# A decaying-attention and two-layer feed-forward kernel on one core: a wider window of loads under way, a state sum moved to a later unit, and a one-product mark for a bank

## The chip, the cores and the metric

The kernel runs on one core of one Trainium2 chip. The metric is the device time of one execution in microseconds (us), given as the median of several runs. One execution was also taken with the hardware profiler, and all rows below come from it. The core's engines work side by side and each takes its instructions in the order in which they are written: TensorE (PE, with PEld for its weight loads), VectorE (DVE), ScalarE (ACT), GpSimd (POOL) and SyncE (SP), which here only issues transfers (DMA).

## The reference, cut to what matters

```python
# attention with decay, per head, in 12 chunks of 64 positions
intra = einsum('bhic,bhjc->bhij', qb, kb) * Dmask            # "scores", masked
intra = einsum('bhij,bhjd->bhid', intra, vb)
inter = einsum('bhid,bhde->bhie', qb * lam_pow, kv_state)
out[:, :, sl] = intra + inter
kv_state = lam_block * kv_state + einsum('bhsd,bhse->bhde', kb * rev_pow, vb)
...
x = out.transpose(0, 2, 1, 3).reshape(1536, 512)
h = x @ w_in;   x = maximum(0.01 * h, h) @ w_out             # 512 -> 2048 -> 512
h = x @ w_in2;  solu = h * softmax(h)                        # 512 -> 1024
y = layernorm(solu) * g_ln @ w_out2                          # 1024 -> 512
```

Everything is float32; the weights come to the kernel as 64-bit words, which it takes apart on the chip.

## The kernel before, in words

**Attention.** The 12 chunks are steps `s` = 0 to 11, two batches together. A step has four groups of 64x64 products on PE: `scores_mm` (line 196), `state_mm` (210), `xs_mm` (250: masked scores times values) and `xq_mm` (264: queries times the state). DVE masks the scores (`scores_ev`, 204) and adds the new state sum to the decayed old state (`state_ev`, 236, reading PSUM bank `aps1`, which is also called `kb`). POOL scales queries (165) and decays the state (190). `alone` writes one group, `both` writes two groups product by product in turn. Steps 0 to 3 run before the feed-forward layer begins; step 4 runs inside its unit 7, step 5 in unit 10 and so on.

**Feed-forward layer 1.** A unit `u` is (token block of 512, feature block of 128). `l1_mm` (439) makes the 128x512 block of h in bank `hps0` or `hps1` by 12 products; `l1_split` puts the leak on it (ACT, 442) and splits it into a high part `ghi` (ACT, 445) and a low part `glo` (DVE, 447); `l2_mm` (456) multiplies both with `w_out` into four banks `acc` by 12 products. PE alternates l1 of unit i and l2 of unit i-1. Scores of the next step are put into the `hps` bank that the next unit's l1 will write.

**Weights.** Pair `n` is one feature block of `w_in` ("IN" half) and the one before it of `w_out` ("OUT" half), 512 KB each. In the first 17 units the pairs are loaded and taken apart while PE uses them. Per pair ACT does `word_hi` (350), `word_lo` (354) and `high` (409); DVE does `clamp` (360), `shift` (370), `join` (379) and `low` (428). In unit i from 4 on the pieces are written so that DVE does clamp and shift of pair i+2, low of pair i+1, `glo` of unit i, then join of pair i+2, and ACT does high of pair i+1, the two steps of `l1_split`, then the words of pair i+3. l1 of unit i needs high and low of pair i.

**Loads.** All weight loads are issued by SP, in order. `load` lets a load go only when, with it, no more than `limit` bytes are under way: it walks back over the earlier loads until their sum exceeds the limit, and waits for that one. Two constants give limits, `AHEAD` (2 MB) and `CALM` (1 MB); loads for attention (`ldw`, `qk`, `kv`) always use `AHEAD`. A load also waits for the readers of the buffer that it fills.

**The mark.** In step 3 the last `xq_mm` of a bank and the first `xs_mm` of it add into the same bank from other rows of the array. `see` therefore lets PE write a few columns of another bank after the `xq_mm` of a bank, lets ACT copy one column of that (244), and `xs_mm` waits for the copy.

`busy(n)` is n products of constants that nobody reads.

Of the kernel before, what the change touches and what calls it, by code (L numbers as in the profile page):

```python
# [10 lines left out]
U32 = mybir.dt.uint32  # L11
# [5 lines left out]
P = 128  # L17
CH = 64
NPAIR = 4
NB = 2  # L20
NPRE = 4
# [3 lines left out]
AHEAD, CALM = 1 << 21, 1 << 20  # L25
# [3 lines left out]
NF = FF1 // P  # L29
# [15 lines left out]
def fused_kernel(ctx: ExitStack, tc: tile.TileContext, att, vt, tab, cst, w_in, w_out, w_in2, w_out2, out):  # L45
# [7 lines left out]
    pe, dve, act, pool, sync = nc.tensor, nc.vector, nc.scalar, nc.gpsimd, nc.sync  # L53
# [10 lines left out]
    aps = [pp.tile([P, 512], F32, name=f"aps{i}") for i in range(2)]  # L64
# [19 lines left out]
    def rows(h):  # L84

        return HALF[1 - h]

    def jrows(s, h):

        return HALF[h] if s < NPRE else HALF[1 - h]  # L90
# [5 lines left out]
    def at(bank, rows, b, pr):  # L96

        if isinstance(bank, tuple):
            return bank[b][rows, pr * CH : (pr + 1) * CH]
        return bank[rows, (b * NPAIR + pr) * CH : (b * NPAIR + pr + 1) * CH]  # L100
# [12 lines left out]
    def load(queue, out, in_, limit=AHEAD):  # L113

        size = 4
        for n in out.shape:
            size *= n
        ins = queue.dma_start(out=out, in_=in_).ins
        ahead = size
        for before, n in reversed(flight):  # L120
            ahead += n
            if ahead > limit:
                tc.add_manual_dep(ins, before.name, SYNC, reason="bytes under way")
                break
        flight.append((ins, size))
# [66 lines left out]
    def scores_mm(s, bank, b, pr):  # L192
        q, k = (qk_t[s][:, :, 0], qk_t[s][:, :, 1]) if s >= NPRE else ld[s][0:2]
        for h in range(2):
            d = rows(h)
            pe.matmul(at(bank, jrows(s, h), b, pr), k[d, b, pr], q[d, b, pr], start=True, stop=True)  # L196
# [41 lines left out]
    LASTPRE, seen, mark = NPRE - 1, {}, tabs[:, 0:NB]  # L238

    def see(s, b):  # L240
        c = (b * NPAIR + NPAIR) * CH - 1
        bank = (aps, hps)[b][0]
        scores_mm(s, bank, b, NPAIR - 1)
        seen[b] = act.copy(mark[:, b : b + 1], bank[:, c : c + 1]).ins

    def xs_mm(s, bank, b, pr):
# [27 lines left out]
    def each_pair(*groups):  # L274

        for pr in range(NPAIR):
            for mm, s, bank, b in groups:
                mm(s, bank, b, pr)

    def alone(mm, s, bank):  # L280
        for b in range(NB):
            each_pair((mm, s, bank, b))

    def both(mm, s, bank, mm2, s2, bank2):
        for b in range(NB):
            each_pair((mm, s, bank, b), *([(mm2, s2, bank2, b)] if s2 < NS else []))

    def step(s, xbank, kbank, rbank):

        both(xs_mm, s, xbank, state_mm, s if s < NS - 1 else NS, kbank)  # L290
        both(xq_mm, s, xbank, scores_mm, s + 1, rbank)
# [5 lines left out]
    def x_hi(s, bank):  # L297
        for src, dst in parts(bank, x_place(s, xhi)):
            act.copy(dst, src)

    def x_lo(s, bank):
        for src, dst, hi in parts(bank, x_place(s, xlo), x_place(s, xhi)):
            dve.tensor_tensor(dst, src, hi.bitcast(F32), op=ALU.subtract)
# [8 lines left out]
    def whole(n):  # L312

        return IN if n == 0 else OUT if n == NF else BOTH

    def load_weights(n, halves=None):
        if n >= len(order):
            return
        kind, f = order[n]
        if n not in raws:  # L320
            if n == NF:
                raws[n] = tmp.tile([P, 1, 512, 2], U32, tag="s", name="rawl")
            else:
                raws[n] = wp.tile([P, 2, 512, 2], U32, tag="w", name="raww")
        t = raws[n]
        if kind == "a":
            load(sync, out=t.rearrange("p h a b -> p (h a b)"), in_=w_in2[f].bitcast(U32))
            return
        halves = halves or whole(n)
        for i in range(halves.start, halves.stop):  # L330
            src = w_out2[f + i] if kind == "b" else w_out[f - 1] if i else w_in[f]
            load(sync, out=t[:, 0 if n == NF else i].rearrange("p a b -> p (a b)"), in_=src.bitcast(U32), limit=(CALM // 2 if n == 1 and i else CALM) if n else AHEAD)

    def of(n, halves):

# [38 lines left out]
    def join(n, halves=None):  # L374
        if n >= len(order):
            return
        raw, x = of(n, halves)
        xu = x.bitcast(U32)
        dve.scalar_tensor_tensor(xu, xu, 0x80000000, raw[:, :, 0], op0=ALU.bitwise_and, op1=ALU.bitwise_or)  # L379
# [19 lines left out]
    def high(n, halves=None):  # L399
        if n >= len(order):  # L400
            return
        kind, f = order[n]
        halves = halves or whole(n)
        t, x = pieces(n), xs_t[n]
        if kind == "b":
            for i in range(2):
                act.activation(t[:, 0, i], x[:, i], AF.Copy, scale=gln[:, f + i : f + i + 1])
        else:
            act.copy(t[:, 0, halves], x[:, halves])  # L409
# [23 lines left out]
    def l1_mm(u, bank):  # L433
        b, f = u
        w = win_t[f].rearrange("p s (k c) -> p s k c", k=KD)
        groups = ((0, xhi), (1, xhi), (0, xlo)) if u == (0, 0) else ((0, xhi), (0, xlo), (1, xhi))
        terms = [(s, k, x) for s, x in groups for k in range(KD)]
        for i, (s, k, x) in enumerate(terms):
            pe.matmul(bank, w[:, s, k], x[b][:, k], start=(i == 0), stop=(i == len(terms) - 1))  # L439
# [136 lines left out]
    c1 = nc.const_aps.tensor(1.0, (P, 1), BF16)  # L576
# [3 lines left out]
    def busy(n):  # L580
        for _ in range(n):
            pe.matmul(aps[0], c1.to_broadcast([P, P]), c1.to_broadcast([P, 512]), start=True, stop=True)
# [30 lines left out]
    xb, sb, kb = acc[0:2], acc[2:4], aps[1]  # L613
# [47 lines left out]
    x3 = (xb[1], hps[1])  # L661
    for b in range(NB):
        each_pair((xq_mm, 3, x3, b))
        see(3, b)
    join(1, IN)
    x_lo(2, xb[0])
    both(xs_mm, 3, x3, state_mm, 3, kb)
    busy(1)
    x_hi(3, x3)
    high(1, IN)  # L670
    x_lo(3, x3)
# [42 lines left out]
    for i, u in enumerate(items[1:], 1):  # L714
        bank = hps[i % 2]
        s = step_at.get(i)
        spare = hps[(i + 1) % 2]
        if i > 1:
            if i == 5:
                alone(scores_mm, NPRE, aps[0])  # L720
            l1_mm(u, bank)
            if s is not None:
                step(s, aps[0], aps[1], spare)
        if i == 2:
            join(3, IN)
            high(3, IN)
            clamp(3, OUT)
            low(3, IN)
            shift(3, OUT)
            l1_split(u, bank)  # L730
            words(4, IN)
            join(3, OUT)
            high(3, OUT)
            clamp(4, IN)
            shift(4, IN)
            low(3, OUT)
            words(4, OUT)
            join(4, IN)
            high(4, IN)
            clamp(4, OUT)  # L740
            shift(4, OUT)
            low(4, IN)
            word_hi(5)
            join(4, OUT)
            word_lo(5)
        elif i == len(items) - 1:
            h2_norm(1, second=lambda: l1_split(u, bank))
        elif i > 2:
            part = OUT if i == 3 else None
            high(pair_at(i, 1), part)  # L750
            clamp(pair_at(i, 2))
            shift(pair_at(i, 2))
            low(pair_at(i, 1), part)
            l1_split(u, bank)
            if s is not None:
                scores_ev(s + 1, spare)
            if i == 6:
                scores_ev(NPRE, aps[0])
                scale_q(NPRE, pool)
                scale_k(NPRE, act)  # L760
            if s is not None:
                state_ev(s, aps[1])
                x_hi(s, aps[0])
                x_lo(s, aps[0])
                load_kv(s + 1)
                load_qk(s + 2)
                scale_q(s + 1, pool)
                decay_state(s + 1, pool)
            if i - 1 in step_at:
                scale_k(step_at[i - 1] + 1, act)  # L770
            join(pair_at(i, 2))
            if i == 4:
                state_ev(NPRE - 1, kb)
            words(pair_at(i, 3))
        load_weights(pair_at(i, 5))
        if i == 2:
            load_kv(NPRE)
            load(sync, out=fix, in_=cst)
            load_qk(NPRE + 1)
        if i == len(items) - 3:  # L780
            h2_norm(0)
            ln_turn(0, on_act=())
        l2_mm(items[i - 1])
        if items[i - 1][1] == NF - 1:
            l2_split(items[i - 1][0])
        if i in h2_after:
            h2_mm(h2_after[i])
# [84 lines left out]
```

## Time and profile before

| what | value |
|---|---|
| median of 3 runs | 447.06 us (445.94 to 447.09) |
| the profiled execution | 445.46 us, span 443.7 us |
| PE busy | 433.7 us (98% of the span) |
| DVE, ACT, POOL busy | 267.3, 195.6, 32.0 us |
| TensorE clock granted | 1.00 (2.4 GHz) in all slices |

The span runs from the first to the last instruction; the profiled execution's own time is 1.8 us longer. A row of a timeline gives the start, the length, the engine, the line of kernel.py, the operation, its output and input tiles, and in brackets how long the engine sat idle before it and what ended that. Rows of equal instructions that follow each other are merged (x12).

### The profile page before, as it was taken

Reading aid. Unit: us, or ns where it says so; the run is one execution under the profiler, and the core shown is the slowest. Engines: PE = TensorE matmul, PEld = TensorE weight load, DVE = VectorE, ACT = ScalarE, POOL = GpSimd, SP = SyncE. Lnnn points to the kernel's source line nnn. Section 1 sums busy time; section 2 is a strip of 40 time slices with the busy share of each in tenths; the row PEclk is TensorE's granted clock in tenths of the full one; section 3 lists DMA queues with packets and bytes.
Section 4 is the critical chain, followed back from the end, with each engine's and each line's share of the span. In section 5 each row is a group of like instructions: output and inputs, shape, how many; then the busy total and the mean of one; then the engine's idle time right before and its main releaser. Section 6 shows DMA issues by size and latency. Waiting matters only on the chain.

```text
span 443.7 us, 8024 instructions
## 1 busy us (share of the span) xinstructions
PE 433.7 (98%) x3270; PEld 356.8 (80%) x3272; DVE 267.3 (60%) x423; ACT 195.6 (44%) x332; POOL 32.0 (7%) x38
## 2 busy tenths in 40 slices
PE   8899998999999999999999999999999999999996
PEld 4788777888888888888888888888888888888886
DVE  4898989999541121211133889716779877777640
ACT  4587866977443222222234778512424322222221
POOL 1500102102201020100000000000000000000000
PEclk9999999999999999999999999999999999999999
DMA  8678788883302030100025542000112222222111
GB/s 296 231 255 260 243 246 236 252 235 98 97 11 87 0 98 0 49 1 0 1 95 188 191 189 96 1 1 10 38 37 72 88 75 73 75 72 74 58 47 47
DMA packets 23699, 46.85 MB, mean 106 GB/s; under 512 B 4336, under 2 KB 12016, under 8 KB 23152
## 3 DMA queue, kind: packets, MB, share of 16 engines
q1 hardware_dynamic: 21792, 44.78, 31.4%
q10 hardware_dynamic: 1872, 1.58, 1.3%
q8 instruction: 25, 0.41, 0.4%
q14 instruction: 10, 0.08, 0.1%
HBM read 37.95 MB, written 3.15 MB: 93 GB/s over the span
## 4 chain that ended last, share of the span: by engine, by line
PE 83%; ACT 0%; issue 0%; DVE 0%
PE acc L456 25%; PE hps L439 25%; PE acc L568 15%; PE aps L476 6%; PE hps L476 5%; PE acc L476 4%; PE aps L250 1%; PE aps L264 1%; PE hps L196 0%; PE aps L210 0%; PE aps L536 0%; PE acc L536 0%; ACT osb L571 0%; DVE state L225 0%
## 5 line engine op out<-in xcount | busy, mean ns | idle before, releaser
L439 PE MATMUL hps<-xhi,wio 128*128 128x512 f32 x384 | 102.9, 390 | 2.7 <-DVE r L204 1.2
L447 DVE TENSOR_TENSOR glo<-hps,ghi 128x512 fp32r<-128x512 f32 x48 | 33.1, 689 | 110.9 <-ACT ghi L445 110.7
L456 PE MATMUL acc<-ghi,wio 128*128 128x512 f32 x384 | 96.1, 392 | 0.6 <-ACT ghi L445 0.6
L439 PEld LDWEIGHTS hps<-xhi,wio 128*128 128x128 f32 x384 | 71.8, 188 | 18.3 <-ACT raww L354 1.6
L456 PEld LDWEIGHTS acc<-ghi,wio 128*128 128x128 f32 x384 | 71.4, 188 | 16.1 <-ACT ghi L445 1.0
L442 ACT ACTIVATE hps<-hps 128x512 f32<-128x512 f32 x48 | 28.0, 584 | 104.9 <-PE hps L439 104.9
L568 PE MATMUL acc<-wb,ln 128*128 128x512 f32 (+1 forms) x312 | 67.6, 373 | 0.0
L568 PEld LDWEIGHTS acc<-wb,ln 128*128 128x128 f32 x312 | 55.3, 188 | 10.2
L439 PE MATMUL hps<-xlo,wio 128*128 128x512 f32 x192 | 51.3, 389 | 0.0
L456 PE MATMUL acc<-glo,wio 128*128 128x512 f32 x192 | 51.3, 389 | 0.0
L439 PEld LDWEIGHTS hps<-xlo,wio 128*128 128x128 f32 x192 | 36.0, 188 | 7.5
L456 PEld LDWEIGHTS acc<-glo,wio 128*128 128x128 f32 x192 | 36.0, 188 | 7.5
L350 ACT ACTIVATE x<-raww 128x1024 f32<-128x1024 f32 (+1 forms) x28 | 27.8, 995 | 11.7 <-DMA raww<-in_w_in_dram 6.6
L379 DVE SCALAR_TENSOR_TENSOR x<-x,raww 128x1024 uint32<-128x1024 uint32 (+1 forms) x28 | 32.2, 1152 | 0.1
L370 DVE SCALAR_TENSOR_TENSOR raww<-x,raww 128x1024 uint32<-128x1024 uint32 (+1 forms) x28 | 29.6, 1056 | 3.8 <-ACT raww L354 1.7
L445 ACT CAST ghi<-hps 128x512 fp32r<-128x512 f32 x48 | 28.2, 587 | 1.5
L354 ACT ACTIVATE raww<-raww 128x1024 uint32<-128x1024 uint16 (+1 forms) x28 | 27.9, 998 | 0.0
L509 POOL TENSOR_TENSOR small<-small,nhalf 128x1 f32<-128x1 f32 x12 | 6.6, 549 | 234.5 <-DVE small L508 234.5
L428 DVE TENSOR_TENSOR wio<-x,wio 128x1024 fp32r<-128x1024 f32 (+1 forms) x21 | 22.2, 1057 | 1.5 <-ACT wio L409 1.5
L409 ACT CAST wio<-x 128x1024 fp32r<-128x1024 f32 (+1 forms) x21 | 17.8, 849 | 11.2 <-DVE x L379 11.2
L165 POOL TENSOR_TENSOR qk<-qk,qpow 128x512 f32<-128x512 f32 x8 | 11.6, 1445 | 140.4 <-PE hps L196 109.6
L571 ACT COPY osb<-acc 128x512 f32<-128x512 f32 (+1 forms) x13 | 7.2, 555 | 32.3 <-PE acc L568 19.5
(115 smaller groups left out, 494.6 us busy)
## 6 DMA issues: line engine op xcount, KB each, us to landing
raww<-in_w_out_dram SPq DMA_DIRECT2D x23, 512.0 KB, 4.3
raww<-in_w_in_dram SPq DMA_DIRECT2D x16, 512.0 KB, 4.3
qk<-in_att_dram SPq DMA_DIRECT2D x8, 512.0 KB, 4.6
raww<-in_w_in_dram SPq DMA_DIRECT2D x4, 1024.0 KB, 4.8
lt<-e SPq DMA_DIRECT2D x124, 32.0 KB, 1.8
out_dram<-osb SPq DMA_DIRECT2D x11, 256.0 KB, 2.2
ldw<-in_att_dram SPq DMA_DIRECT2D x7, 384.0 KB, 5.4
kv<-in_att_dram SPq DMA_DIRECT2D x16, 128.0 KB, 3.4
```

The lines of the kernel that those rows point to most:

```text
L350: act.activation(x, raw[:, :, 1].bitcast(F32), AF.Copy, scale=HI_SCALE)
L354: act.activation(raw[:, :, 0], raw.bitcast(U16)[:, :, 1], AF.Copy, scale=LO_SCALE)
L370: dve.scalar_tensor_tensor(raw[:, :, 0], x.bitcast(U32), 3, raw[:, :, 0], op0=ALU.logical_shift_left, op1=ALU.bitwise_or)
L379: dve.scalar_tensor_tensor(xu, xu, 0x80000000, raw[:, :, 0], op0=ALU.bitwise_and, op1=ALU.bitwise_or)
L428: dve.tensor_tensor(t[:, 1, halves], x[:, halves], t[:, 0, halves].bitcast(F32), op=ALU.subtract)
L439: pe.matmul(bank, w[:, s, k], x[b][:, k], start=(i == 0), stop=(i == len(terms) - 1))
L442: act.activation(bank, bank, AF.Prelu, alpha=0.01)
L445: act.copy(ghi, bank)
L447: dve.tensor_tensor(glo, bank, ghi.bitcast(F32), op=ALU.subtract)
L456: pe.matmul(acc[m], w[:, s, m], g, start=(f == 0 and first), stop=(f == NF - 1 and last))
L476: pe.matmul(bank, x[b][:, k, o : o + P], w2_t["a", k, half][:, s], start=(i == 0), stop=(i == len(terms) - 1),)
L568: pe.matmul(po[:, 0:n], x[:, k], w2_t["b", k][:, s, cols], start=(i == 0), stop=(i == len(terms) - 1))
```

## The change: what it does

Three edits. Weight loads of pair 3 and later (the pairs count from 0) get the limit of 2 MB, where those of pair 1 and later had 1 MB (the second half of pair 1 has 512 KB in both). `see` writes its mark by one product of constants, 128x64 in bfloat16, where it repeated one pair's two score products. `state_mm` of step 3 is written beside the scores of step 4 in unit 5, where it stood beside `xs_mm` of step 3 before the first unit; one `busy` product there is gone; and `state_ev` of step 3 stands in unit 6, where it stood in unit 4.

```diff
     def see(s, b):
-        c = (b * NPAIR + NPAIR) * CH - 1
+        c = CH - 1
         bank = (aps, hps)[b][0]
-        scores_mm(s, bank, b, NPAIR - 1)
+        pe.matmul(bank[:, 0:CH], c1.to_broadcast([P, P]), c1.to_broadcast([P, CH]), start=True, stop=True)
         seen[b] = act.copy(mark[:, b : b + 1], bank[:, c : c + 1]).ins
...
-            load(sync, ..., limit=(CALM // 2 if n == 1 and i else CALM) if n else AHEAD)
+            load(sync, ..., limit=CALM // 2 if n == 1 and i else CALM if n in (1, 2) else AHEAD)
...
-    both(xs_mm, 3, x3, state_mm, 3, kb)
-    busy(1)
+    alone(xs_mm, 3, x3)
...
             if i == 5:
-                alone(scores_mm, NPRE, aps[0])
+                both(scores_mm, NPRE, aps[0], state_mm, NPRE - 1, kb)
...
-            if i == 4:
+            if i == 6:
                 state_ev(NPRE - 1, kb)
```

On SP the order of the loads stays; the waits move. The piece below begins at the first half of pair 3 (`raww`), with the semaphore of an earlier transfer behind "waits".

```order
-L118 DMA raww<-in_w_in_dram 128x1024 [waits DMAHW2_49,DMAHW0_49]
-L118 DMA raww<-in_w_out_dram 128x1024 [waits DMAHW3_49,DMAHW1_49]
-L118 DMA qk<-in_att_dram 128x2x512
-L118 DMA raww<-in_w_in_dram 128x1024 [waits DMAHW5_49,DMAHW3_49]
+L118 DMA raww<-in_w_in_dram 128x1024 [waits DMAHW2_49]
+L118 DMA raww<-in_w_out_dram 128x1024 [waits DMAHW3_49]
+L118 DMA qk<-in_att_dram 128x2x512 [waits DMAHW0_49]
+L118 DMA raww<-in_w_in_dram 128x1024 [waits DMAHW5_49,DMAHW1_49]
```

Pair 3 no longer waits for the two halves of pair 2 (DMAHW0 and DMAHW1); the load of `qk` and the first half of pair 4 do, so each load may go out two loads sooner.

On DVE, from `glo` of unit 4 on, with join (L379), clamp (L360) and shift (L370); further down the rows are those of unit 6, where L204 is the mask of step 4's scores:

```order
 L447 TENSOR_TENSOR glo<-hps_83,ghi 128x512
 L379 SCALAR_TENSOR_TENSOR x<-x,raww 128x1024
-L236 TENSOR_TENSOR state<-aps_86,sd 128x512
 L360 TENSOR_SCALAR x<-x 128x1024
 L370 SCALAR_TENSOR_TENSOR raww<-x,raww 128x1024
...
 L204 TENSOR_TENSOR r<-aps_85,dmask 128x512
 L379 SCALAR_TENSOR_TENSOR x<-x,raww 128x1024
+L236 TENSOR_TENSOR state<-aps_86,sd 128x512
 L360 TENSOR_SCALAR x<-x 128x1024
```

The state's addition now stands after join of unit 6, the last DVE work before that of unit 7, whose step 4 multiplies with this state and writes its own sum into the same bank.

## Rows read from the trace of the kernel before

**Rows 1.** Windows: span, PE, PEld, DVE, ACT, POOL busy, clock, DMA share, GB/s.
```profile
4.00:14.00 10.00, 9.14 (x225) 5.86 (x224) 6.66 (x19) 3.46 (x8) 2.28 (x2) 1.00 1.01 380
23.20:42.60 19.40, 19.38 (x85) 16.07 (x86) 18.26 (x33) 16.03 (x28) 0.00 (x0) 1.00 0.78 251
42.60:71.20 28.60, 25.87 (x256) 20.30 (x254) 25.52 (x29) 23.58 (x32) 3.76 (x2) 1.00 0.81 243
71.40:430.00 358.60, 358.60 (x2353) 297.23 (x2354) 207.91 (x333) 143.42 (x243) 20.75 (x24) 1.00 0.25 78
```

**Rows 2.** Timeline of PE: the idle times, scores of step 4, step 4.
```profile
21.60 0.27 PE L250 MATMUL acc<-r,ldw 64*64 64x64 f32 x2 [1.07 <-ACT tabs L244]
...
23.22 2.11 PE L439 MATMUL hps<-xhi,wio 128*128 128x512 f32 x8 [0.46 <-ACT xhi L299]
...
45.83 2.11 PE L456 MATMUL acc<-ghi,wio 128*128 128x512 f32 x8 [0.56 <-ACT ghi L445]
...
48.78 1.15 PE L196 MATMUL aps<-qk 64*64 64x64 f32 x32
...
62.06 1.19 PE L439 MATMUL hps<-xhi,wio 128*128 128x512 f32 x4 [1.03 <-ACT wio L409]
...
65.01 0.27 PE L250 MATMUL aps<-r,kv 64*64 64x64 f32 x2
...
65.99 0.22 PE L264 MATMUL aps<-qk,state 64*64 64x64 f32 x2
...
71.30 1.15 PE L439 MATMUL hps<-xhi,wio 128*128 128x512 f32 x4 [1.25 <-DVE r L204]
```

**Rows 3.** Timeline of ACT: word_hi (L350) where a load was awaited, the mark's copy.
```profile
19.79 0.68 ACT L350 ACTIVATE x<-raww 128x512 f32<-128x512 f32 x1 [1.53 <-DMA raww<-in_w_in_dram]
...
21.39 0.16 ACT L244 COPY tabs<-aps 128x1 f32<-128x1 f32 x1
...
27.93 0.67 ACT L350 ACTIVATE x<-raww 128x512 f32<-128x512 f32 x1
...
41.99 1.14 ACT L350 ACTIVATE x<-raww 128x1024 f32<-128x1024 f32 x1 [0.99 <-DMA raww<-in_w_out_dram]
...
46.39 1.16 ACT L350 ACTIVATE x<-raww 128x1024 f32<-128x1024 f32 x1 [0.61 <-DMA raww<-in_w_out_dram]
...
58.92 1.12 ACT L350 ACTIVATE x<-raww 128x1024 f32<-128x1024 f32 x1 [3.45 <-DMA raww<-in_w_out_dram]
```

**Rows 4.** Timeline of DVE from 43 to 71 us: its idle times, step 3's state, unit 7.
```profile
43.16 0.69 DVE L360 TENSOR_SCALAR x<-x 128x1024 f32<-128x1024 f32 x1 [0.49 <-ACT x L350]
44.20 1.23 DVE L370 SCALAR_TENSOR_TENSOR raww<-x,raww 128x1024 uint32<-128x1024 uint32 x1 [0.35 <-ACT raww L354]
...
53.15 0.68 DVE L236 TENSOR_TENSOR state<-aps,sd 128x512 f32<-128x512 f32 x1
...
60.08 0.69 DVE L360 TENSOR_SCALAR x<-x 128x1024 f32<-128x1024 f32 x1 [1.47 <-ACT x L350]
61.11 1.23 DVE L370 SCALAR_TENSOR_TENSOR raww<-x,raww 128x1024 uint32<-128x1024 uint32 x1 [0.34 <-ACT raww L354]
...
64.59 1.22 DVE L379 SCALAR_TENSOR_TENSOR x<-x,raww 128x1024 uint32<-128x1024 uint32 x1
...
67.64 2.31 DVE L428 TENSOR_TENSOR wio<-x,wio 128x1024 fp32r<-128x1024 f32 x1
...
70.48 0.67 DVE L204 TENSOR_TENSOR r<-hps,dmask 128x512 f32<-128x512 f32 x1
```

**Rows 5.** Timeline of SP: the second half of pair 2 is issued; of POOL: unit 7.
```profile
23.22 0.33 SPq L118 DMA_DIRECT2D raww<-in_w_out_dram  x1
...
67.24 1.64 POOL L165 TENSOR_TENSOR qk<-qk,qpow 128x512 f32<-128x512 f32 x1 [15.10 <-PE hps L196]
```

**Rows 6.** DMA issues of the page: count, KB each, median us from issue to landing.
```profile
raww<-in_w_in_dram SPq DMA_DIRECT2D x16, 512.0 KB, 4.3
...
ldw<-in_att_dram SPq DMA_DIRECT2D x7, 384.0 KB, 5.4
```

More of the change, by code (lines that the diff above doesn't have):

```diff
@@ L331, in load_weights @@
             src = w_out2[f + i] if kind == "b" else w_out[f - 1] if i else w_in[f]
-            load(sync, out=t[:, 0 if n == NF else i].rearrange("p a b -> p (a b)"), in_=src.bitcast(U32), limit=(CALM // 2 if n == 1 and i else CALM) if n else AHEAD)
+            load(sync, out=t[:, 0 if n == NF else i].rearrange("p a b -> p (a b)"), in_=src.bitcast(U32), limit=CALM // 2 if n == 1 and i else CALM if n in (1, 2) else AHEAD)
     def of(n, halves):
```

## The prediction

> **What bounds the kernel now.** I read the windows first. From 71.40 to 430 us PE is busy in all 358.60 of 358.60 us [rows 1]: nothing that moves other engines there can shorten the run, and whatever PE gains before 71 us is kept to the end. From 23.20 to 42.60 us PE is busy in 19.38 of 19.40 us. The stretch between, 42.60 to 71.20 us, has PE busy in only 25.87 of 28.60 us [rows 1]. So the change is decided there and in the first 23 us.
>
> The timeline of PE names the idle times [rows 2]: 1.07 us before the first `xs_mm` of step 3 (the mark's copy on ACT), 0.46 us before the first l1 (ACT's `x_hi`), then 0.56 us at 45.83 (`ghi` of unit 3 from ACT), 1.03 us at 62.06 (`high` of pair 7 from ACT) and 1.25 us at 71.30 (DVE has not yet taken the scores of step 5 out of the bank that l1 of unit 8 writes). The last three make 2.84 us.
>
> Why were ACT and DVE late? ACT's timeline shows three `word_hi` that waited for the second half of a weight pair: 0.99, 0.61 and 3.45 us, those of pairs 5, 6 and 8 [rows 3]. ACT takes its work in order, so `ghi` of unit 3 stood behind the first of these and `high` of pair 7 behind the last. DVE is the other engine with almost no air: it was busy in 25.52 of the 28.60 us [rows 1], and of the 3.08 us idle, 0.49, 0.35, 1.47 and 0.34 us (2.65) stand just behind ACT's word steps of pairs 5 and 8 [rows 4]. So all three idle times of PE have one root, loads that landed late; the third comes by way of DVE, whose chain was held up and reaches the scores of step 5 at 70.48 us [rows 4].
>
> **Part 1, the wider window.** Can the loads be faster? With 1 MB under way the chip moved 251 and 243 GB/s in the two stretches; in the start, where the limit is 2 MB, it moved 380 GB/s from 4 to 14 us, at a DMA share of 1.01 against 0.78 and 0.81 [rows 1]. I take 380. How early does pair 8, the worst one, then come? From the second half of pair 2 (issued at 23.22 us [rows 5]) to the second half of pair 8 there are 13 halves and two `qk` of 0.524 MB, and `kv` and `fix` with 0.59 MB by their shapes: 8.45 MB. At 247 GB/s that is 34.2 us, so 57.4 us; the trace has 58.92. At 380 GB/s it is 22.2 us, so 45.5 us. ACT was free for it at 58.92 - 3.45 = 55.47 us, and up to 1.6 us earlier if the waits of pairs 5 and 6 go too. The point from which the wait is gone is therefore 8.45 MB in 30.7 us, 275 GB/s. Pair 5 is wanted at 41.0 us; 4.19 MB at 380 GB/s are there at 34.3. All three waits of ACT go, with much to spare. Buffers don't hold the loads back: pairs 10 and 11 fill buffers of pairs 2 and 4, whose join DVE has done before it comes to pair 5 at 43.16 us [rows 4], and the next `kv` must wait for step 4 as before.
>
> What is late next? I walk the three engines to unit 8. PE: without 0.56 and 1.03, it would come to l1 of unit 8 at 71.30 - 1.25 - 1.59 = 68.46 us. DVE: its chain to the scores of step 5 is one unbroken row of work once the idle times are out; 70.48 - 2.65 to 2.9 gives 67.6 to 67.8 us, end of the evacuation 68.3 to 68.5. The two meet, so the third idle time goes nearly whole. Term: **-2.84 us**; bounds -1.59 (the third wait stays whole) and -3.2 (each restart of PE after a wait also costs some 0.1 us, estimated from 2.11 and 1.15 us of the first rows after a wait).
>
> **Part 2, step 3's sum.** 32 score products alone took 1.15 us [rows 2]; in step 4 the 64 of `both` took 65.99 - 65.01 = 0.98 us. Products written in turn lie side by side on the array, so state products beside `xs_mm` cost next to nothing, and beside the scores in unit 5 next to nothing again. Term 0, bounds -0.1 and +1.0 (as if they cost 0.98 us by themselves). The `busy` product that goes lay in the 0.46 us in which PE waited for ACT: 0; if that cover were gone, a gain of under 0.3 us.
>
> `state_ev` is another matter. It leaves DVE 0.6 us earlier at 53.15 us and comes back behind join of unit 6. Step 4's first `state_mm` writes the bank that it reads, and stands second in PE's queue there; behind it are all of step 4 and l2 of unit 6. In the trace join of unit 6 starts at 64.59 us [rows 4]; less 2.65 and 0.6 it is 61.34, its end about 62.5, the sum done at 63.2 us. PE reaches step 4 at 65.01 - 1.59 = 63.42 us. So the new wait is 0 by a margin of 0.2 us, and a wait up to about as long as what is left of PE's third idle time is absorbed there, since DVE's own row of work decides that. Term 0, bounds 0 and +0.7.
>
> **Part 3, the mark.** PE waited for ACT's copy at 21.39 us, and ACT came to it only after its words of pair 1, whose load landed at 19.79 us [rows 3]; that load keeps its limit. The products of the mark stand in PE's queue ahead of that idle time in either form. Term 0, bounds -0.4 and +0.2.
>
> **Against it.** A wider window makes each load slower to land: 5.4 us in the start, with 2 MB under way, against 4.3 us with 1 MB [rows 6]. That matters for one load alone, the second half of pair 2, issued just before the extra ones: 23.22 + 4.3 = 27.5 us, and ACT takes it at 27.93 without a wait [rows 3]; with 5.4 us it is 28.6, 0.7 us late, and DVE, with 1.14 us idle in 19.40 [rows 1], could make up little of it. I take 0, since that load is issued ahead of them, and keep +0.7 for the range. The Trainium skill ("DMA: Bandwidth & Descriptors", Latency and other measured facts) speaks against the change here: HBM's access latency is 0.2 us on average but 2 us at high load. By that, as an estimate, the load would land up to 1.8 us later, at 29.3 us, and 1.4 us of the gain would go; no row here shows a latency by itself.
>
> Sum: -2.84 us. The profiled execution took 445.46 us; it would take 442.6. The median of the runs, 447.06, lies 1.6 above the profiled one; from it the sum gives 444.2. If the loads' lateness is what differs between runs, the changed kernel comes nearer to 442.6 in all of them; I say **443.7 us**.
>
> **Rivals.**
> 1. *DVE keeps the bound* (0.15). The first two idle times go, but the scores of step 5 are taken out later than I reckon. For it: `low` of pair 8 took 2.31 us at 67.64 while POOL scaled queries for 1.64 us from 67.24 [rows 4, 5], and shifted work may meet POOL's twice. Then the gain is 1.59 to 2.0 us: 445.3. The Trainium skill ("GPSIMD Engine Reference", Specifications) says the same of the cause: GpSimd shares its SBUF interfaces with VectorE, and instructions with two SBUF inputs contend. The trace agrees (2.31 us beside 1.2 for its neighbours of the same size).
> 2. *The loads are not faster* (0.08). If something other than the window holds the rate at 250 GB/s, ACT's waits stay. Then the moved sum ends at 66.4 us where PE stands at 65.01, and DVE comes to the scores 0.65 us later: 447.7. Against it: 380 GB/s in the start.
> 3. *Slower* (0.07). The extra loads share the engines with the second half of pair 2. Each microsecond that it lands after 27.93 us is passed on through ACT and DVE. It eats the whole gain at 2.84 us late (7.5 us to landing) and makes the kernel slower by over 0.3% (1.34 us) at 4.2 us late, 8.9 us to landing; the nearest row has 5.4. At 9.2 us: 448.7.
>
> **How the numbers follow.** My forecast has 0.70, with its own range 442.4 to 444.9. The range that should hold 8 in 10 reaches over rival 1 and the bounds +0.7: 442.2 to 446.0. A measurement of this kernel can tell about 0.3%, 1.34 us. Faster: nearly all of 0.70 and most of 0.15, together 0.81; same: rival 2 and the edges, 0.13; slower: 0.06.
>
> **What would show it.** Right: no ACT `word_hi` waits for a load between 40 and 70 us; the DMA rate between 25 and 45 us is above 330 GB/s; PE idle from 42 to 71 us falls from 2.7 to under 0.6 us; l1 of unit 8 starts near 68.4 us. Wrong: `word_hi` of pair 2 waits at 27.9 us, or PE waits for L236 at step 4 by more than 0.5 us while l1 of unit 8 still waits for DVE, or PE shows new idle time after 71 us.

## The result and the profile after

The changed kernel took 441.94 us (441.40 to 442.18, 4 runs) where the kernel before took 447.07 us (445.94 to 447.27, 4 runs). The ratio is 0.9889, with a 95% interval of 0.9869 to 0.9908: faster by 1.1%. I had said faster, at 443.7 us with a range from 442.2 to 446.0; the time lies 0.26 us below the range. The profiled execution took 441.72 us (span 439.9 us), 3.74 us less than that of before.

The windows of the changed kernel (span, PE, PEld, DVE, ACT, POOL busy, clock, DMA share, GB/s) answer to [rows 1]:

```profile
4.00:14.00 10.00, 9.33 (x214) 5.59 (x214) 6.53 (x19) 4.72 (x12) 3.81 (x3) 1.00 1.01 379
...
23.20:42.60 19.40, 19.40 (x87) 16.02 (x86) 18.26 (x33) 17.04 (x29) 0.00 (x0) 1.00 0.95 350
42.60:71.20 28.60, 28.60 (x303) 23.57 (x302) 28.05 (x35) 23.38 (x32) 4.95 (x3) 1.00 0.66 228
71.40:426.00 354.60, 354.60 (x2337) 293.90 (x2336) 203.55 (x326) 142.07 (x242) 19.68 (x23) 1.00 0.23 74
```

PE is busy all the time from 23.2 to 426 us, where 2.73 us were idle between 42.6 and 71.2 us before. The loads ran at 350 GB/s instead of 251 from 23.2 to 42.6 us. The next stretch moves less because the loads are so far ahead by then that they wait for buffers: none goes out between 53.23 and 63.96 us, where `kv` must wait for the `state_mm` of step 4. DVE's idle time in that next stretch fell from 3.08 to 0.55 us.

PE's timeline in the changed kernel, against [rows 2]: the mark, the first l1, l2 of unit 3, l1 of unit 7, step 4, l1 of unit 8.

```profile
21.27 0.68 PE L250 MATMUL acc<-r,ldw 64*64 64x64 f32 x16 [0.53 <-ACT tabs L244]
...
22.89 2.12 PE L439 MATMUL hps<-xhi,wio 128*128 128x512 f32 x8 [0.47 <-ACT xhi L299]
...
44.80 1.98 PE L456 MATMUL acc<-ghi,wio 128*128 128x512 f32 x8
...
59.72 1.07 PE L439 MATMUL hps<-xhi,wio 128*128 128x512 f32 x4
...
62.54 0.33 PE L250 MATMUL aps<-r,kv 64*64 64x64 f32 x4
...
67.65 1.07 PE L439 MATMUL hps<-xhi,wio 128*128 128x512 f32 x4
```

No idle time stands before the last four. The 3.8 us of the span add up from these rows: the first l1 begins 0.33 us earlier (22.89 against 23.22), from there to l1 of unit 8 it is 44.76 us instead of 48.08, which is 3.32 less, and behind it 0.15 us less. Of the 3.32, the three idle times are 2.84. The other 0.48 are what is left of two things. In an unbroken row four products follow the four before them by 0.91 us though a row is given as 1.07 us long, since the next one begins before the last has ended. A wait loses these 0.16 us of overlap, and behind it the first products also stand up to 0.14 us further apart, so each of the three restarts cost 0.23 to 0.30 us beside its idle time, 0.74 of them in this stretch. Against that, step 4 took 2.22 us where it took 2.03, and a few rows some 0.01 to 0.03 us more.

ACT's timeline, against [rows 3]: `word_hi` of pair 2's second half, of pair 5 and of pair 8.

```profile
27.61 0.67 ACT L350 ACTIVATE x<-raww 128x512 f32<-128x512 f32 x1
...
40.56 1.17 ACT L350 ACTIVATE x<-raww 128x1024 f32<-128x1024 f32 x1
...
53.96 1.16 ACT L350 ACTIVATE x<-raww 128x1024 f32<-128x1024 f32 x1
```

DVE's timeline, against [rows 4]: step 3's state, `low` of pair 8 and the scores of step 5.

```profile
61.96 0.68 DVE L236 TENSOR_TENSOR state<-aps,sd 128x512 f32<-128x512 f32 x1
...
64.48 1.22 DVE L428 TENSOR_TENSOR wio<-x,wio 128x1024 fp32r<-128x1024 f32 x1
...
66.21 0.68 DVE L204 TENSOR_TENSOR r<-hps,dmask 128x512 f32<-128x512 f32 x1
```

Behind 23 us no `word_hi` waits for a load. DVE has the scores of step 5 out at 66.9 us, 0.76 us before PE wants their bank; before, PE waited 1.25 us for that.

### The profile page after: what moved, and what is told of

It is laid out like the page before. It is cut to its first block, busy times and chain, and to the rows that moved or that the text cites. A ratio compares the mean times of both kernels' runs of the same rounds, so it can differ in the third digit from the quotient of the medians.

```text
span 439.9 us, 8003 instructions
## 1 busy us (share of the span) xinstructions
PE 433.7 (99%) x3264; PEld 357.2 (81%) x3265; DVE 265.0 (60%) x423; ACT 195.6 (44%) x332; POOL 32.3 (7%) x38
## 3 DMA queue, kind: packets, MB, share of 16 engines
q10 hardware_dynamic: 1872, 1.58, 1.2%
## 4 chain that ended last, share of the span: by engine, by line
PE 94%; DMA 4%; ACT 1%; issue 0%; SPq 0%
PE acc L456 30%; PE hps L439 30%; PE acc L568 15%; PE aps L476 6%; PE hps L476 5%; PE acc L476 4%; DMA ldw<-in_att_dram 3%; PE aps L250 2%; PE aps L264 1%; DMA raww<-in_w_in_dram 1%; PE aps L210 1%; PE hps L196 0%; PE aps L196 0%; PE aps L536 0%; PE acc L536 0%; ACT x L350 0%
## 5 line engine op out<-in xcount | busy, mean ns | idle before, releaser
L370 DVE SCALAR_TENSOR_TENSOR raww<-x,raww 128x1024 uint32<-128x1024 uint32 (+1 forms) x28 | 29.5, 1055 | 3.0 <-ACT raww L354 0.4
L379 DVE SCALAR_TENSOR_TENSOR x<-x,raww 128x1024 uint32<-128x1024 uint32 (+1 forms) x28 | 31.3, 1118 | 0.1
L350 ACT ACTIVATE x<-raww 128x1024 f32<-128x1024 f32 (+1 forms) x28 | 27.9, 998 | 6.5 <-DMA raww<-in_w_in_dram 6.5
L428 DVE TENSOR_TENSOR wio<-x,wio 128x1024 fp32r<-128x1024 f32 (+1 forms) x21 | 20.9, 994 | 1.7 <-ACT wio L409 1.7
```

The source lines that it names most:

```text
L350: act.activation(x, raw[:, :, 1].bitcast(F32), AF.Copy, scale=HI_SCALE)
L370: dve.scalar_tensor_tensor(raw[:, :, 0], x.bitcast(U32), 3, raw[:, :, 0], op0=ALU.logical_shift_left, op1=ALU.bitwise_or)
L428: dve.tensor_tensor(t[:, 1, halves], x[:, halves], t[:, 0, halves].bitcast(F32), op=ALU.subtract)
```

## The experiments

Theory A: the gain is the loads, which land in time; mark and moved sum are worth next to nothing. Rival B: mark or moved sum carry a good part. Later runs ask how much window is needed and what a still wider one costs.

**1. The window alone.** In the kernel before, only this line changes:

```diff
-limit=(CALM // 2 if n == 1 and i else CALM) if n else AHEAD
+limit=CALM // 2 if n == 1 and i else CALM if n in (1, 2) else AHEAD
```

> The kernel before with the wider window of loads alone (2 MB from pair 3 on); mark, products and state sum as before. Theory A (all of the gain is the loads): 441.9 to 442.4 us, no PE idle time from 42 to 71 us above 0.2 us, no ACT wait for a load there. Theory B (mark and moved sum carry a good part, 1 us or more of the 5.1 us): 443 us or more.

Measured: 441.65 us (441.17 to 442.18, 6 runs) against 445.34 us for the kernel before on the same chip (443.26 to 449.24, 29 runs); ratio 0.9908 (0.9873 to 0.9942). Its window from 42.6 to 71.2 us:

```profile
42.60:71.20 28.60, 28.60 (x272) 23.54 (x271) 28.06 (x35) 23.26 (x32) 5.11 (x3) 1.00 0.67 234
```

That is the changed kernel's time: Theory A. The gain is 3.7 us here where the first comparison had 5.1; the kernel before is what differs, 445.34 us in 29 runs against 447.07 in 4.

**2. Mark and sum without the window.** The changed kernel with the old line for the limit.

> The changed kernel with the old window (1 MB): mark, products and sum moved, loads as before. Theory A: the ACT waits stay; the sum of step 3 now ends on DVE at about 66.4 us where PE stands at about 65 us, so PE waits some 1.4 us for L236 or for the sum in step 4, and l1 of unit 8 starts about 0.65 us later than before: 447.1 to 448.2 us against 447.1. Theory B: 446 us or less.

Measured: 446.25 us (443.58 to 448.39, 12 runs), ratio 1.0013 (0.9984 to 1.0042). No gain, and no loss that can be told; the median lies between the two theories' numbers, and Theory A's 447.1 us did not come. Since this kernel and the one before both spread over some 5 us, the medians can't carry half a microsecond either way. The profiled execution took 447.44 us: ACT waited 9.5 us for loads between 23 and 72 us.

**3. The sum alone.** As run 2, with the old mark.

> The kernel before with the sum of step 3 moved alone (products beside the scores of step 4, the filler product gone, the addition in unit 6); old mark, old window. Theory A: as the run with mark and sum, 447.1 to 448.2 us, the mark being worth under 0.2 us. Theory B (the mark is worth something): the two differ by more than 0.5 us.

Measured: 446.03 us (443.39 to 448.09, 12 runs), ratio 1.0015 (0.9987 to 1.0042), 0.2 us from run 2: the mark is worth nothing that can be measured, though the median lies 1.1 us below the range given. The trace shows what the moved sum does when the loads are late. PE's timeline of this run at step 4:

```profile
67.25 0.27 PE L210 MATMUL aps<-kv 64*64 64x64 f32 x2 [1.12 <-ACT raww L354]
```

DVE's timeline of this run, the sum of step 3:

```profile
66.46 0.68 DVE L236 TENSOR_TENSOR state<-aps,sd 128x512 f32<-128x512 f32 x1
```

PE waits 1.12 us at the first `state_mm` of step 4. The row puts the wait down to an ACT instruction, but DVE's sum ends at 67.14, and PE goes on at 67.25: it is the bank that the sum reads. In return the wait for the scores of step 5 is gone from the list of PE's waits. The new wait took the place of the old one, as rival 2 of the prediction has it.

**4. The kernel before, again.**

> The kernel before, unchanged, profiled once more, to see what differs between its runs (445.46 in the profiled one, 445.94 to 447.27 in the others). Theory A (the loads' lateness differs): if this execution is the longer one, ACT waits longer for loads between 40 and 70 us, and PE's idle time there is longer by the difference, 0.5 to 1.7 us; the time from 72 us to the end is the same within 0.2 us. Theory C (the start or the end differs): PE's idle time from 42 to 71 us is 2.7 to 3.0 us again, and the difference stands before 23 us or after 430 us.

Measured: 444.83 us (443.63 to 448.07, 10 runs); the profiled execution took 444.76 us, 0.70 less than the 445.46 of the first. Its window from 42.6 to 71.2 us and its first l1:

```profile
42.60:71.20 28.60, 25.79 (x254) 19.88 (x254) 26.36 (x31) 22.63 (x31) 2.93 (x2) 1.00 0.77 251
...
22.10 2.11 PE L439 MATMUL hps<-xhi,wio 128*128 128x512 f32 x8
```

PE was idle for 2.81 us in that stretch, against 2.73, and ACT waited 5.6 us for loads, against 5.1. The first l1 began at 22.10 us instead of 23.22, and from there to the end this execution took 0.4 us longer. So between these two it is Theory C: the start differs. Among other executions with 1 MB the loads' lateness differs too: 3.40 us (run 3) and 4.90 us (run 2) of idle PE go with 446.21 and 447.44 us. And all kernels with 1.5 MB or more from pair 3 on and the old limits before that, which have no such idle time, lie between 441.1 and 444.0 us, most of them below 442.5. So the kernel before is spread by both, its start and the lateness of its loads.

**5. One and a half megabytes.**

```diff
-... CALM if n in (1, 2) else AHEAD
+... CALM if n in (1, 2) else 3 << 19 if n else AHEAD
```

> The changed kernel with 1.5 MB instead of 2 MB from pair 3 on. The point from which ACT's waits are gone was put at 275 GB/s on the stretch from 23 to 54 us. Theory A (rate grows with the bytes under way, 250 GB/s at 1 MB and 350 at 2 MB): about 300 GB/s, above that point, so ACT's waits are gone or under 1 us in sum and the time is 441.5 to 443 us, with a spread of runs under 1.5 us. Theory B (2 MB is needed for the chip to keep its pace): rate under 275 GB/s, ACT waits of 2 us or more, 443.5 us or more and a spread of several us.

Measured: 441.73 us (441.08 to 442.80, 6 runs), ratio 0.9911 (0.9880 to 0.9942). The window of 23.2 to 42.6 us:

```profile
23.20:42.60 19.40, 19.40 (x87) 16.05 (x86) 18.25 (x33) 17.02 (x30) 0.00 (x0) 1.00 0.92 319
```

319 GB/s, above the 275 that the prediction's point of decision asks for, and no ACT wait for a weight load behind 23 us: Theory A. Its runs spread over 1.7 us, a little more than the 1.5 expected. One more half megabyte is enough.

**6. Two megabytes for pairs 1 and 2 too.**

```diff
-limit=CALM // 2 if n == 1 and i else CALM if n in (1, 2) else AHEAD
+limit=AHEAD
```

> The changed kernel with 2 MB for all pairs, 1 and 2 too (pair 1's second half had 512 KB, the rest of pairs 1 and 2 had 1 MB). Theory A (transfers are served in the order of issue): pair 1's first half is issued near 11 us instead of 16, lands before ACT wants it at 18.2 us, the mark's copy comes 0.3 to 0.9 us earlier, and the time falls by 0.2 to 0.6 us from the changed kernel's 441.7 to 441.1 to 441.6; pair 2 lands no later. Theory S (transfers under way share the engines): the attention inputs of step 3 or the first halves of pairs 1 and 2 land later than before, ACT waits more before 30 us, and the time is 442.5 us or more.

Measured: 442.60 us (441.46 to 446.80, 12 runs), ratio 0.9929 (0.9903 to 0.9955). Theory S has the time but not the cause: pair 1 goes out at 13.04 us instead of 16.06, ACT waits for it 0.33 us instead of 1.26, and yet the lower runs are no better than the changed kernel's. The profiled execution took 446.80 us. Its PE timeline in step 3:

```profile
20.69 1.65 PE L196 MATMUL acc<-ldw 64*64 64x64 f32 x25 [3.38 <-issue]
```

Its windows (columns as above) during that idle time, from the fall of the clock on, and behind that:

```profile
17.30:20.70 3.40, 0.03 (x3) 0.01 (x2) 2.01 (x3) 2.30 (x5) 1.36 (x2) 0.85 0.95 310
19.70:26.40 6.70, 5.71 (x95) 5.35 (x97) 3.02 (x5) 1.04 (x4) 0.00 (x0) 0.50 0.94 320
26.50:27.00 0.50, 0.50 (x22) 0.50 (x22) 0.00 (x0) 0.00 (x0) 0.00 (x0) 1.00 0.64 246
```

PE sits idle for 3.38 us in the middle of the scores of step 3 with no semaphore awaited ("issue"), and then runs at half its clock (0.50, that is 1.2 GHz) until 26.4 us, for 5.7 us. In other kernels PE also pauses between the same two products, for 0.36 us in the changed kernel.

**7. POOL's scaling later.** In the kernel before, the two calls on POOL in a step change places.

```diff
-                scale_q(s + 1, pool)
                 decay_state(s + 1, pool)
+                scale_q(s + 1, pool)
```

> The kernel before (1 MB) with POOL's scaling of the queries written behind its decay of the state, so that it runs after DVE has taken out the scores of step 5. Theory A (the wait at l1 of unit 8 came in part from POOL lying beside DVE's low of pair 8, 2.31 us instead of 1.22): that low takes 1.2 to 1.3 us and the wait for the scores falls from 1.25 to under 0.4 us. Theory B: low stays near 2.3 us or the wait stays near 1.2 us. The whole time says little, since runs of this kernel spread over 6 us.

Measured: one execution, 444.32 us. DVE's timeline of unit 7:

```profile
67.41 1.22 DVE L428 TENSOR_TENSOR wio<-x,wio 128x1024 fp32r<-128x1024 f32 x1
...
69.15 0.68 DVE L204 TENSOR_TENSOR r<-hps,dmask 128x512 f32<-128x512 f32 x1
```

PE's timeline at l1 of unit 8:

```profile
69.98 1.16 PE L439 MATMUL hps<-xhi,wio 128*128 128x512 f32 x4
```

`low` of pair 8 takes 1.22 us instead of 2.31, and of the wait for the scores 0.14 us is left: Theory A. So 1.09 of the 1.25 us of that wait came from POOL lying beside this one instruction. The loads were no earlier in this execution: ACT waited 5.1 us for them between 23 and 72 us, as long as in the first execution of the kernel before.

**8. Three megabytes** from pair 3 on (`3 << 20 if n else AHEAD` in the place of `AHEAD`).

> The changed kernel with 3 MB instead of 2 MB from pair 3 on. Theory A (at 2 MB the transfer engines are full, 0.95 of their time, and serve in order of issue): rate as at 2 MB within 8%, each load lands later (7 to 9 us instead of 5.7), ACT waits for none, time 441.2 to 442.2 us. Theory S (transfers under way share the engines, so more of them delay each): ACT waits for loads between 27 and 40 us and the time rises above 442.5 us.

Measured: 441.87 us (441.36 to 444.02, 9 runs), ratio 0.9921 (0.9893 to 0.9949). 371 GB/s from 23.2 to 42.6 us, 7.0 and 7.4 us from issue to landing, no ACT wait for a load behind 23 us: Theory A. The profiled execution, 444.02 us, was its longest. It waited for the mark 1.17 us, for a load of pair 1, and then lost time at the first l1. Its windows:

```profile
21.00:23.80 2.80, 1.18 (x33) 1.01 (x32) 2.53 (x5) 1.99 (x8) 0.00 (x0) 1.00 0.87 312
23.80:27.30 3.50, 3.49 (x8) 2.76 (x9) 3.27 (x7) 3.16 (x6) 0.00 (x0) 0.52 0.87 327
```

PE was busy in 1.18 of 2.80 us, and then had half the clock (0.52) for 3.5 us: eight products took 3.68 us, where the changed kernel's took 2.12. In run 7 PE was as idle before its first l1 (with more products in its row), and the clock stayed:

```profile
20.75:23.55 2.80, 1.16 (x65) 1.12 (x66) 2.55 (x5) 1.98 (x8) 0.00 (x0) 1.00 0.90 310
23.55:27.05 3.50, 3.50 (x15) 2.92 (x16) 3.25 (x8) 3.13 (x6) 0.00 (x0) 1.00 0.78 242
```

**9. Two megabytes for pair 2** (`CALM if n == 1 else AHEAD`), pair 1 as in the changed kernel.

> The changed kernel with 2 MB for pair 2 too (pair 1 keeps 1 MB and 512 KB). With 2 MB for pairs 1 and 2 one execution showed PE idle for 3.4 us at 17.3 us with nothing awaited but its own instructions, in a stretch in which the loads took 0.95 of the transfer engines and no instruction load was served. Theory I (PE's instructions queue behind loads under way when those fill the engines between 14 and 20 us): here the engines stay part idle until 20 us, so no such wait over 0.7 us, 441.2 to 442.3 us and a spread under 1.5 us. Theory P (chance, or pair 2's loads): a wait over 1 us or runs above 443.5 us here too.

Measured: 442.15 us (441.50 to 443.08, 10 runs), ratio 0.9930 (0.9898 to 0.9962). PE's longest pause for its own instructions was 0.91 us, a little over what Theory I allows, with the transfer engines at 0.42 of their time from 17 to 20 us. The times fit Theory I; the 0.91 us doesn't quite, and the spread of 1.58 us is a little over the 1.5 expected.

**10. Two megabytes for pair 1** (`CALM if n == 2 else AHEAD`).

> The changed kernel with 2 MB for pair 1 (pair 2 keeps 1 MB). Theory I: pair 1's halves go out near 13 and 14 us and are followed by pair 2's, which fills the engines from 14 to 20 us; PE waits for its instructions by 1 us or more in some executions, and some runs lie above 443.5 us. Theory P: no such wait, 441.2 to 442.3 us.

Measured: 441.95 us (441.41 to 445.39, 10 runs), ratio 0.9938 (0.9906 to 0.9971). The profiled execution took 443.81 us. Its PE timeline, with the two pauses:

```profile
15.10 0.92 PE L196 MATMUL acc<-ldw 64*64 64x64 f32 x25 [1.45 <-issue]
...
20.21 0.97 PE L196 MATMUL acc<-ldw 64*64 64x64 f32 x25 [2.00 <-issue]
```

Its windows from 14 to 20 us:

```profile
14.00:17.00 3.00, 1.90 (x69) 1.90 (x72) 1.17 (x3) 0.14 (x2) 1.35 (x3) 1.00 1.04 386
17.00:20.00 3.00, 1.21 (x71) 1.07 (x66) 2.34 (x4) 3.00 (x8) 2.51 (x2) 1.00 0.49 164
```

Pauses of 1.45 and 2.00 us, as Theory I expects; but the longer one falls at 18.2 us, when the engines were back to half their time. Theory I also had pair 2's loads fill the engines until 20 us, which they didn't: they went out only from 18.68 us on.

**11. Experiment 6 once more.**

> The kernel with 2 MB for all pairs, profiled once more. Theory I: if the time is above 443.5 us, PE has again an idle time of over 1 us with no semaphore awaited, between the score products of step 3, and its granted clock falls behind it; if it is below 442 us, that idle time is under 0.7 us. Theory P: a long execution shows its extra time elsewhere.

Measured: one execution, 441.08 us, with one pause of 0.73 us (Theory I had put it under 0.7), and the transfer engines at 0.95 and 0.99 of their time from 14 to 20 us:

```profile
14.00:17.00 3.00, 2.64 (x117) 2.41 (x113) 2.84 (x5) 2.13 (x8) 2.85 (x3) 1.00 0.95 338
17.00:20.00 3.00, 2.63 (x80) 2.53 (x82) 2.64 (x4) 2.51 (x6) 1.47 (x2) 1.00 0.99 356
```

So full engines do not by themselves make the long pause. Among these executions pauses of over 1 us between score products come only with the wide early window: 3.38, 2.00 and 1.45 us there, under 1 us with the old limit of pair 1.

What PE waits for there can be seen in queue q8, which loads instructions, 16 KB at a time. In the changed kernel such loads end at 12.63 and 16.25 us, and PE ends its two pauses in the score products at 14.02 and 17.49. In run 10 they end at 13.83 and 18.81 us, and the pauses at 15.10 and 20.21; in run 6 the second one is served from 18.29 to 19.25 us, and the pause ends at 20.69. (So an instruction load was served within that pause, though the expectation of run 9 says none was.) PE goes on 1.2 to 1.5 us after the load each time, so by these times the long pauses are waits for late instruction loads. What made these late is open: that they queue behind the weight loads is argued, not shown, and in run 11 the load came at 14.96 us in spite of full engines.

None of the eleven runs beats the changed kernel by more than their spread.

## Why the prediction was right in its cause and wrong in its numbers

**The loads were the cause: shown.** The window alone gives the whole gain (run 1), mark and sum none that can be told (runs 2 and 3). The start of a run varies, so it is clearer still from the first l1 to the end of the span: 420.5 and 420.9 us in the two executions of the kernel before, 416.8 with the window alone, 417.0 to 417.1 in the changed kernel and in runs 5, 6, 9, 10 and 11 (run 8 had half the clock there). The rate in the stretch is 350 GB/s where I took 380, and 319 GB/s was enough (run 5); the point of 275 itself was not tried.

**PE's three idle times go: right.** All of the -2.84 us came. That all three have one root was too simple for the third: in run 7 the loads were as late as before, and that wait went when POOL's scaling was moved. It took both, late loads and the meeting with POOL.

**The size of the sum was too small.** The step that failed is the term "-2.84 us; bounds -1.59 and -3.2", and with it "each restart of PE after a wait also costs some 0.1 us", which I left in the bound instead of the sum. Each restart cost 0.23 to 0.30 us: I compared only the lengths of the first rows after a wait and overlooked the 0.16 us of overlap that is lost ahead of it. Between the first l1 and l1 of unit 8 the change was -3.32: 0.48 more than the idle times, where my bound left room for 0.36. So l1 of unit 8 began at 67.65 us and not near 68.4. The rest of the 3.74 us, 0.33 at the start and 0.09 beyond, lies outside that stretch: ACT had the load of pair 1 at 19.45 us instead of 19.79, with the same limit as before. No edit explains that, and the two executions of the kernel before differ by 1.12 us there, so this part of the time was luck. From the profiled execution my sum gave 442.6, and 441.72 came.

**The reference was the other half of the miss.** I set the prediction between 442.6 (from the profiled execution) and 444.2 (from the median), though I wrote that if the loads' lateness is what differs between runs, the changed kernel comes nearer to 442.6 in all of them. That was so. The runs of the kernel before in the three later comparisons (29, 22 and 19 of them) lie between 442.5 and 449.2 us, with medians of 445.34, 445.74 and 444.76, so the 447.06 of 3 runs was high, and its runs spread over 1.5%, where I took 0.3% as what a measurement can tell. The 4 runs of the changed kernel lie between 441.4 and 442.2. A wait on a late load varies; when it is hidden, that variation goes with it, and the kernel comes out near its best, not at its median less the gain. The range's lower end, 442.2, stood 0.4 us below a sum that was itself 0.9 us too small.

**Rival 1, DVE keeps the bound: did not happen,** and my walk was too slow there. I reckoned the scores of step 5 out at 68.3 to 68.5 us, just about when PE comes; they were out at 66.9. POOL's scaling runs beside `low` of pair 8 again, but now DVE's instruction began first, at 64.48 us. POOL's timeline in the changed kernel:

```profile
64.91 1.95 POOL L165 TENSOR_TENSOR qk<-qk,qpow 128x512 f32<-128x512 f32 x1 [14.12 <-PE hps L196]
```

`low` took 1.22 us and POOL's scaling 1.95, where before POOL began first and took 1.64, and DVE's took 2.31 [rows 4, 5]. Run 7 shows by itself that this one meeting made 1.09 us. By the Trainium skill ("GPSIMD Engine Reference", Specifications) GpSimd shares its SBUF interfaces with VectorE, and they contend where VectorE's instruction has two SBUF inputs, as `low` has. Both traces agree, 2.31 us in one and 1.95 in the other. The prediction did not foresee that the order would turn; DVE was first by only 0.43 us. Had POOL been first again, 1.09 us more would have made a wait of some 0.3 us, an estimate from the 0.76 us of room.

**Step 3's sum:** PE entered step 4 at 62.54 us and the sum ended at 62.64, so the margin of 0.2 us was a wait of about 0.1, and step 4 took 2.22 us instead of 2.03. The term that I put at 0 is therefore +0.2; run 1, where the sum is not moved, took 2.03 us in step 4. With late loads the wait is 1.12 us (run 3), where 1.4 was worked out. The products cost nothing in either place: in the changed kernel the `xs_mm` of step 3 alone hold PE as long as they did with the state products between them (1.14 and 1.17 us).

**The mark: nothing,** as said; PE went on 0.20 us after ACT's copy began (21.07 and 21.27 us) as it did before (21.39 and 21.60).

**The warning did not come true.** SP's timeline in the changed kernel, the second half of pair 2 and the load that waits for it, the first half of pair 4:

```profile
22.99 0.33 SPq L118 DMA_DIRECT2D raww<-in_w_out_dram  x1
...
26.94 0.34 SPq L118 DMA_DIRECT2D raww<-in_w_in_dram  x1
```

That is at most 3.95 us to landing, with three loads (1.5 MB) issued behind it; before, the second half of pair 3 waited for the same load and went out at 27.17 us, 3.95 us after 23.22. Loads issued later did not slow it, which speaks for service in the order of issue and against rival 3. The Trainium skill's 2 us of latency at high load ("DMA: Bandwidth & Descriptors", Latency and other measured facts) gave 29.3 us as an estimate; the measurement decides, and the load was there by 26.94. Loads issued into a full window do take longer, 5.6 and 5.8 us in the changed kernel from 23.2 to 42.6 us instead of 4.1 and 4.4.

## What to carry to other kernels

Where an engine in the middle of a chain waits for loads and the transfer engines are part idle, look at the bytes under way before anything else: here 1 MB gave 250 GB/s, 1.5 MB 319, 2 MB 350, 3 MB 371, and the second step of half a megabyte already bought no time. When a wait on a varying thing is removed, work the prediction from the least disturbed execution, not from the median of a few, and price a wait with what its restart costs: here 0.23 to 0.30 us beside the idle time. And a limit that looks too cautious can guard something else: widening it for the first pairs too brought long runs back.

## What was not expected of the hardware

PE can sit idle for its own instructions: 3.38 us in run 6 and 2.00 us in run 10, between the same two products at which it pauses 0.36 us in the changed kernel. Both came where loads had been let out early. Within the 3.38 us, and after a stretch with PE busy in 1.18 of 2.80 us in run 8, the granted clock fell to half (0.50 and 0.52 in their rows), until 26.4 and 27.3 us. After the 2.00 us of run 10 it stayed at 1.00 from 20.2 to 26 us, and after 1.16 of 2.80 us in run 7 as well. What decides it stays open.
